# Two-layer gated network behind top-32 attention on one Trainium2 core: softmax weights turned by a transposing DMA, and five chunks instead of six

## The chip, the core and the metric

The program runs on one core of a Trainium2 chip. The metric is the device time of one execution in microseconds, the median of several runs. The engines are named as the profile has them: PE (TensorE, with PEld for its weight loads), DVE (VectorE), ACT (ScalarE), POOL (GpSimd) and SP (SyncE, which here issues every DMA).

## The reference

For 4 batches, 8 heads, 576 positions and a head width of 64, each row of scores keeps its 32 largest values and takes a softmax over them; the result is multiplied with v. The 2304 tokens of width 512 then go through two gated networks of inner width 1536, the first with silu, the second with a sigmoid as its gate.

```python
scores = scale * np.matmul(q, k.transpose(0, 1, 3, 2))
kth = np.partition(scores, -top_k, axis=-1)[..., -top_k:-top_k + 1]
scores = np.where(scores >= kth, scores, -1000000000.0)
attn = softmax(scores); x = np.matmul(attn, v)
g = x @ w_gate; x = (silu(g) * (x @ w_val)) @ w_out
x = (sigmoid(x @ w_gate2) * (x @ w_val2)) @ w_out2
```

## The kernel before, in words

The 36 units of 64 query positions (9 in each batch) are cut into chunks by `SIZES`, before `[4, 5, 6, 7, 7, 7]`; a chunk has an attention part (`attention`, `segment`) and a feed-forward part (`moe`). Heads go in four pairs. In `segment` two units of one batch make a *pair of row tiles*: two tiles of 128 rows by 576 scores, one for each head. A unit left over makes one tile (m = 1).

For each row tile `row_tile` finds the 32 largest values on DVE (`top_full`: four MAX8, three MATCH_REPLACE8), takes the exponent on ACT, and normalises on ACT or POOL. The weights `p` are then turned for the product with v: `turned` (L893) has PE transpose five 128-column blocks of a tile into PSUM (nine blocks for a pair), and ACT copies them into `pt` (L930). `pv` (L934) multiplies; PE's `ps_v` matmuls are the weighted sums. `pt` has one buffer (`PT = 1`).

Chunk 0 is in mode N: its feed-forward part multiplies in plain fp32, and its weights come from DRAM as 64-bit values, which `decode` (L513) turns to fp32 on ACT, POOL and DVE in four steps (L521 to L554). Every decoded piece is also stored to DRAM (`sw`, L557). All other chunks are in mode P: `slab` (L570) loads a decoded piece of weights again (`raw`), and `split_ops` (L497) splits it into a rounded high part (ACT or POOL) and a rest (POOL); activations are split likewise. Each product then takes three matmuls, high by high, high by rest and rest by high. A feed-forward part of a chunk in mode P is 864 matmuls over as many columns as the chunk has tokens, 64 for each unit. Its scores come from `stacked` and `stacked_scores` (L675), which stack high parts and rests, from pair of heads 1 of chunk 2 on; ahead of that, scores are plain fp32 (`score_ops`, L692).

The order on each engine is fixed in advance: `Plan` (L135) holds every operation with its estimated duration and a priority from the tables at the head of the file, places them one after another, and the program is then emitted in that order. So each engine, and SP's DMA queue, works strictly in order. Buffers are rings (`Ring`), and an operation that takes a buffer waits until its last user is done.

Of the kernel before, what the change touches and what calls it, by code (L numbers as in the profile page):

```python
# [9 lines left out]
F32 = mybir.dt.float32  # L10
# [42 lines left out]
DL = 6
NA = [0, 2, 3.5, 3.5, 4.0, 3.5]
NP = [1, 1, 1, 0, 2, 0]
P_XC = [0, 1, 0.5, 1, 0, 1]
P_EV = [0.5, 2, 1, 1, 1, 1]
D_WR = 10.5
D_ST = 5.5
D_RAW = [6, 4, 2.5, 0, 0, 0]  # L60
D_K = [0, 1, 1, 2, 0, 1]
D_V = [3.5, 1, 5.5, 3.5, 1, 3.5]
P_ROUND = [4, 4, 6, 4, 4, 4]
P_MASK = [0, 2, 0, 1, 1, 1]
P_DEC = 1.0
# [5 lines left out]
P_EX = [3.5, 3.5, 1.5, 2.5, 0, 0]
P_S = [0, 0, 0.5, 0.5, 1.5, 1.5]
P_X = [2, 2.5, 0.5, 1.5, 3.0, 1.5]
P_HH = [0, 0, 2.5, 0, 1.0, 2.0]
P_HL = [3, 1.5, 0, 0, 2, 1]
# [264 lines left out]
def attn_moe_kernel(ctx: ExitStack, tc, qT, kT, qD, kD, vL, wall, outT):  # L340
# [52 lines left out]
    def home(nm, dtype=F32):  # L393
# [5 lines left out]
        "x32": ring("x32", [P, NPAIR, S], F32, 1),  # L399
# [7 lines left out]
        "pt": ring("pt", [P, 9, 64 * GMAX], F32, PT),  # L407
        "v": ring("v", [P, 10, D], F32, V_RING),
# [56 lines left out]
    R["se", 0] = slot("xs", [P, 2, 2, 288], F32, 2)  # L465
    last = PHASE[-1]
    R["w", last] = Ring(lambda nm: [home(f"w_{4 * int(nm.split('_')[1]) + i}", F32R) for i in range(4)], WF // 4)
    R["w", last].before = lambda i: [g for k in range(4) for g in R["wf", 0].last(4 * i + k)]
    R["raw", last] = slot(lambda i: f"wr{i}" if i < WR else f"wu{i - WR}", [P, 512], F32, WR + WU)
    R["raw", last].before = lambda i: R["wr", 0].last(i) if i < WR else R["wu", 0].last(i - WR)  # L470
# [99 lines left out]
    def slab(c, i):  # L570

        mode, ph = MODES[c], PHASE[c]
        mode = {"a": "PS", "b": "SR"}.get(mode, mode * 2)[i % 2]
# [10 lines left out]
        w = new(("w", ph))  # L584

        def part(a, x):
            return w[2 * a + x][:].rearrange("p (a b) -> p a b", b=P)

        def block(x):
            return lambda a, d: part(a, x)[:, d]  # L590
        out = []
        for x in range(2):
            if mode == "R":
                ops = []
                for a in range(2):
                    def fn(a=a, x=x):
                        take(w)
                        nc.sync.dma_start(f32(part(a, x)), parts[i][a, x].rearrange("p (a b) -> p a b", b=P))
                    ops.append(op("dma", dma(128 * 2048), fn, deps=[kept[i][a, x]], allocs=[w], prio=4, lat=DMA_LAT))
                out.append((block(x), w, ops))  # L600
                continue
            r = new(("raw", ph))
            ld = load(r, scr32[i][:, x], n_bytes=128 * 2048, prio=D_RAW[now[0]], deps=stored[i])
            ops = split_ops(lambda x=x: part(0, x), lambda x=x: part(1, x),
                            lambda r=r: r[:].rearrange("p (a b) -> p a b", b=P), 512, [r], [ld], 2, 2, allocs=[w])
            for a in range(2 * (mode == "S")):
                def fn(a=a, x=x):
                    nc.sync.dma_start(parts[i][a, x].rearrange("p (a b) -> p a b", b=P), f32(part(a, x)))
                kept[i][a, x] = op("dma", dma(128 * 2048), fn, deps=[ops[a]], uses=[w], prio=6, lat=DMA_LAT)
            out.append((block(x), w, list(ops)))  # L610
# [23 lines left out]
    def stacked(bp, q0, n):  # L634
# [20 lines left out]
        lds.append(op("dma", dma(P * n * 256), fn, deps=lds, uses=[qr], prio=1, lat=DMA_LAT))  # L655
# [113 lines left out]
    def segment(c, p, b, q0, n_s, x32g, col, held=None):  # L769
# [123 lines left out]
    def turned(pg, norms, ptg, c0, k3, m):  # L893
# [39 lines left out]

    def pv(ptg, pt_ops, vg, v_ld, n, p, x32g, col):  # L934
# [232 lines left out]
```

## Time and profile before

| | |
|---|---|
| median of 3 runs | 1261.97 us (1261.35 to 1262.12) |
| the profiled execution | 1261.78 us, of which 1260.0 us are the span |
| PE, PEld busy | 1212.7 us (96%), 1060.8 us (84%) |
| DVE, ACT, POOL busy | 855.5, 874.7, 1047.0 us (68%, 69%, 83%) |
| DMA | 200.37 MB, mean 159 GB/s |
| clock granted to TensorE | 0.995 of full |

Times are counted from the start of the span. A busy time is the union of an engine's instructions, so neighbours that overlap count once. In a timeline row the start is measured, while ends of matmuls are modelled: the price of a matmul in a row of others is read from start to start. Register, semaphore and DMA-issuing instructions are not counted as busy.

### The profile page before, as it was taken

How to read it: one execution, taken by the hardware profiler on the slowest of the kernel's cores; microseconds unless marked ns; L12 is line 12 of the kernel's file. 1: busy time of each engine (PE TensorE's matmuls, PEld its weight loads, DVE VectorE, ACT ScalarE, POOL GpSimd, SP SyncE). 2: the span in 40 equal slices, each digit the busy share in tenths (PEclk: the TensorE clock that was granted, in tenths of full speed). 3: DMA queues.
4: the chain of work that ended last, by engine and by line, in shares of the span. 5: the costliest groups of instructions: out<-in, count | busy, mean ns of one | idle time of the engine just before them, and what ended most of it. 6: DMA issues, size and time to landing. Idle time of an engine off the chain costs nothing. (4 is left out here: it accounts for less than half of the span.)

```text
span 1260.0 us, 21906 instructions
## 1 busy us (share of the span) xinstructions
PE 1212.7 (96%) x7288; PEld 1060.8 (84%) x7288; DVE 855.5 (68%) x1872; ACT 874.7 (69%) x1886; POOL 1047.0 (83%) x1134
## 2 busy tenths in 40 slices
PE   4798999999999999999999999999999999999998
PEld 1376767879989899999998889999888899999998
DVE  6999999946999989999877999801968010121110
ACT  5998999967998999889888875434787433232331
POOL 5777989989999999979898887897887589787883
PEclk9899999999999999999999999999999999999999
DMA  7877788886444463544454464234232234333231
GB/s 262 261 265 255 256 279 273 265 261 192 139 150 142 135 209 114 163 132 142 129 169 139 142 220 152 98 121 131 78 105 68 84 105 137 112 112 117 100 106 41
DMA packets 100913, 200.37 MB, mean 159 GB/s; under 512 B 12480, under 2 KB 22848, under 8 KB 100800
## 3 DMA queue, kind: packets, MB, share of 16 engines
q1 hardware_dynamic: 100800, 198.98, 49.6%
q8 instruction: 57, 0.93, 0.3%
q14 instruction: 56, 0.46, 0.1%
HBM read 171.21 MB, written 27.72 MB: 158 GB/s over the span
## 5 line engine op out<-in xcount | busy, mean ns | idle before, releaser
L506 POOL TENSOR_TENSOR w<-raw,w 128x512 fp32r<-128x512 f32 x360 | 462.0, 1294 | 18.0 <-ACT w L501 5.6
L984 PE MATMUL ps_m<-xh,w 128*128 128x448 f32 (+2 forms) x1920 | 402.4, 351 | 1.5 <-DVE sil L955 1.4
L984 PEld LDWEIGHTS ps_m<-xh,w 128*128 128x128 f32 x1920 | 336.4, 188 | 21.2 <-issue 2.5
L882 DVE MAX8 st<-wk 128x8 f32<-128x576 f32 x432 | 313.2, 748 | 0.9
L984 PE MATMUL ps_m<-xl,w 128*128 128x448 f32 (+2 forms) x960 | 216.8, 347 | 0.0
L884 DVE MATCH_REPLACE8 wk<-st,wk 128x576 f32<-128x576 f32 x288 | 213.1, 742 | 0.0
L984 PE MATMUL ps_m<-hh,w 128*128 128x448 f32 (+2 forms) x960 | 199.2, 349 | 0.0
L984 PEld LDWEIGHTS ps_m<-xl,w 128*128 128x128 f32 x960 | 172.2, 187 | 8.7
L984 PEld LDWEIGHTS ps_m<-hh,w 128*128 128x128 f32 x960 | 168.8, 188 | 7.8 <-issue 0.4
L501 ACT ACTIVATE w<-raw 128x512 fp32r<-128x512 f32 x247 | 150.7, 625 | 20.2 <-PE ps_m L984 8.2
L506 POOL TENSOR_TENSOR hl<-h,hh 128x448 fp32r<-128x448 f32 (+2 forms) x120 | 128.8, 1074 | 5.6 <-ACT hh L501 5.0
L501 ACT ACTIVATE hh<-h 128x448 fp32r<-128x448 f32 (+2 forms) x116 | 62.9, 542 | 101.0 <-DVE h L955 67.8
L503 POOL TENSOR_SCALAR w<-raw 128x512 fp32r<-128x512 f32 x113 | 69.9, 619 | 67.1 <-PE ps_m L984 66.5
L842 ACT ACTIVATE e<-s,st 128x576 f32<-128x576 f32 x144 | 110.0, 771 | 19.8 <-DVE st L882 19.4
L955 DVE SCALAR_TENSOR_TENSOR h<-sil,ps_m 128x448 f32<-128x448 f32 (+2 forms) x60 | 34.5, 575 | 130.9 <-PE ps_m L984 126.6
L955 DVE SCALAR_TENSOR_TENSOR sil<-sil,ps_m 128x448 f32<-128x448 f32 (+4 forms) x83 | 40.6, 490 | 120.7 <-ACT sil L1019 120.7
L882 DVE MAX8 st<-s 128x8 f32<-128x576 f32 x144 | 106.0, 747 | 20.9 <-ACT s L702 20.8
L924 PE MATMUL ps_t<-ident,p 128*128 128x128 f32 x656 | 103.1, 284 | 16.9 <-POOL p L864 9.4
L930 ACT ACTIVATE pt<-ps_t 128x512 f32<-128x512 f32 (+4 forms) x288 | 112.2, 419 | 9.4 <-PE ps_t L924 7.8
L924 PEld LDWEIGHTS ps_t<-ident,p 128*128 128x128 f32 x656 | 76.8, 143 | 43.8 <-POOL p L864 19.8
L846 ACT ACTIVATE p<-e,st 128x576 f32<-128x576 f32 x144 | 110.8, 771 | 1.4 <-POOL st L837 0.6
L1019 ACT ACTIVATE sil<-ps_m 128x448 f32<-128x448 f32 (+4 forms) x155 | 71.6, 462 | 54.0 <-PE ps_m L984 53.5
(67 smaller groups left out, 1870.9 us busy)
## 6 DMA issues: line engine op xcount, KB each, us to landing
raw<-sw SPq DMA_DIRECT2D x360, 256.0 KB, 2.9
wr<-in_wall_dram SPq DMA_DIRECT2D x72, 512.0 KB, 4.8
sw<-wf SPq DMA_DIRECT2D x72, 256.0 KB, 3.2
kr<-in_kD_dram SPq DMA_DIRECT2D x42, 288.0 KB, 2.9
v<-in_vL_dram SPq DMA_DIRECT2D x34, 320.0 KB, 3.9
ss<-se SPq DMA_DIRECT2D x6, 576.0 KB, 3.6
s<-ss SPq DMA_DIRECT2D x6, 576.0 KB, 4.5
k<-in_kT_dram SPq DMA_DIRECT2D x11, 288.0 KB, 3.7
```

The costliest lines, as they stand in the source:

```text
L501: nc.scalar.activation(out=hi(), in_=raw(), func=AF.Copy)
L503: nc.gpsimd.tensor_scalar(hi(), raw(), 1.0, 1.0, op0=ALU.mult, op1=ALU.mult)
L506: (nc.gpsimd if eng == "pool" else nc.vector).tensor_sub(lo(), (lo_raw or raw)(), lo_hi() if lo_hi else f32(hi()))
L842: nc.scalar.activation(out=eg[:], in_=src(), func=AF.Prelu, bias=stg[:, 31:32], scale=-1.0, alpha=1.0 / STEEP)
L846: nc.scalar.activation(out=pg[:, e * S:(e + 1) * S], in_=eg[:], func=AF.Exp, bias=stg[:, 32:33], scale=-STEEP, accum_out=stg[:, 33:34])
L882: nc.vector.max(out=stg[:, 4 * k:4 * k + 8], in_=src() if k == 0 else fresh[:])
L884: nc.vector.match_replace(out=fresh[:], in_to_replace=stg[:, 4 * k - 4:4 * k + 4], in_values=src() if k == 1 else fresh[:], imm_value=NEG)
L924: nc.tensor.transpose(tg[:width, i], pg[:, a:a + width], ident)
L930: nc.scalar.activation(out=dst(), in_=src(), func=AF.Copy)
L955: nc.vector.scalar_tensor_tensor(out=out, in0=t, scalar=1.0, in1=x, op0=ALU.add, op1=ALU.mult)
L984: nc.tensor.matmul(pg[:, :n], blk(a, d), src(x, d), start=first and i == 0, stop=last and i == 4 * len(terms) - 1)
L1019: nc.scalar.activation(out=sg[:, :n], in_=pg[:, :n], func=AF.Tanh, scale=0.5)
```

## The change

Three things change together, and the tables of priorities with them.

**Chunks.** `SIZES` becomes `[4, 8, 8, 8, 8]`. Chunk 0 stays; then come four chunks of 512 tokens instead of five of 320, 384 and three times 448. A feed-forward part in mode P is run four times instead of five.

**Weights' buffers.** `raw` is loaded once for both halves of a slab (512 KB, ring of 3), and the split weights lie in a ring of `WH = 7` halves, each half a buffer of its own. The rings `sil`, `h32` and `wk` have one buffer fewer each.

**Turning.** From the third chunk on (`XT = "00111"`) a pair of row tiles is not turned on PE. `crossed` copies its fp32 weights on DVE, ACT or POOL into two planes of 16-bit halves, stores these to DRAM, and loads them back into `pt` by a DMA with `transpose=True`, which puts the two halves of each value next to each other again. A row tile left alone (m = 1) is turned as before. The blocks of `pt` are renumbered (0 to 3, 5 to 8, the shared one 4). 44 pairs are crossed: 16, 12 and 16 in chunks 2, 3 and 4.

```diff
-SIZES = [4, 5, 6, 7, 7, 7]
+SIZES = [4, 8, 8, 8, 8]
-MODES = "NPPPPP"
+MODES = "NPPPP"
-EARLY = '000002'
+EARLY = '00001'
-P_PT = [0.5, 3.5, 2.5, 2.5, 2.5, 5.5]
-P_PV = [1.5, 1, 0, 2, 0, 0]
+P_PT = [2.5, 3.5, 1.5, 1.5, 1.5, 4.5]
+P_PV = [1, 0, 0, 2, 0, 0]
...
-SIL = 4
-H32 = 3
-WK = 3
+WH = 7
+SIL = 3
+H32 = 2
+WK = 2
...
+XT = "00111"
+XT_NS = 4000.0
+PL = {'dve': (1270, 5), 'act': (1365, 6), 'pool': (1230, 4)}
+PL_DMA = 3.5
+PL_RING = 1
...
+        "pl": ring("pl", [P, 2 * S], F32, PL_RING, dt=I16),
...
-        w = new(("w", ph))
+        r = new(("raw", ph))
+        ld = load(r, scr32[i], n_bytes=128 * 4096, prio=D_RAW[now[0]], deps=stored[i])
         for x in range(2):
-            r = new(("raw", ph))
-            ld = load(r, scr32[i][:, x], n_bytes=128 * 2048, prio=D_RAW[now[0]], deps=stored[i])
+            w = new(("w", ph))
...
+                if XT[c] == "1" and m == 2:
+                    pt_ops.append(crossed(pg, norms, ptg, 2 * jp * 64))
+                    continue
                 for k3 in range(m + 1):
                     pt_ops += turned(pg, norms, ptg, 2 * jp * 64, k3, m)
...
+    def crossed(pg, norms, ptg, c0):
+        plg = new("pl")
+        scr = drp.tile([P, 2, 2 * S], I16, tag=plg.name, name=f"sp_{plg.name}")
+        ops = []
+        for e, d in enumerate(norms):
+            def plane(eng, e=e):
+                take(plg)
+                o = plg[:][:, :, e * S:(e + 1) * S]
+                i = pg[:, e * S:(e + 1) * S].bitcast(I16).rearrange("p (k t) -> p t k", t=2)
+                if eng == "act":
+                    nc.scalar.activation(out=o, in_=i, func=AF.Copy)
+                elif eng == "dve":
+                    nc.vector.tensor_copy(o, i)
+                else:
+                    nc.gpsimd.tensor_copy(o, i)
+            ops.append(op(PL, 0, plane, deps=[d], uses=[pg], allocs=[plg]))
+        def st():
+            nc.sync.dma_start(scr, plg[:])
+        a = op("dma", dma(P * 2 * S * 4), st, deps=ops, uses=[plg], prio=PL_DMA, lat=DMA_LAT)
+        def tr():
+            take(ptg)
+            nc.sync.dma_start(ptg[:, :, c0:c0 + P].bitcast(I16), scr.rearrange("q t k -> (q t) k"), transpose=True)
+        return op("dma", XT_NS, tr, deps=[a], allocs=[ptg], prio=PL_DMA, lat=DMA_LAT)
```

**The order on three engines.** In the rows below a name's number is that of its buffer's use, `x4` the number of like instructions in a row.

PE in the middle of chunk 1's second network, beside which the attention of chunk 2 runs (`ps_t` a transpose, `ps_m` a feed-forward product, `ps_v` a weighted sum). Before:

```order
490 L924 MATMUL ps_t_4897<-ident,p_4803 128x128 x4
491 L984 MATMUL ps_m_4906<-xh_4039,w_4643 128x320 x4
492 L984 MATMUL ps_m_4906<-xh_4039,w_4645 128x320 x4
493 L984 MATMUL ps_m_4906<-xl_4040,w_4643 128x320 x4
494 L924 MATMUL ps_t_4933<-ident,p_4803 128x128 x4
495 L984 MATMUL ps_m_4942<-xh_4039,w_4644 128x320 x4
496 L984 MATMUL ps_m_4942<-xh_4039,w_4646 128x320 x4
497 L984 MATMUL ps_m_4942<-xl_4040,w_4644 128x320 x4
498 L924 MATMUL ps_t_4963<-ident,p_4803 128x128
499 L984 MATMUL ps_m_4965<-xh_4039,w_4747 128x320 x4
```

and in the changed program:

```order
491 L1018 MATMUL ps_m_5260<-xh_4611,w_w_5013 128x512 x4
492 L1018 MATMUL ps_m_5260<-xh_4611,w_w_5014 128x512 x4
493 L1018 MATMUL ps_m_5260<-xl_4612,w_w_5013 128x512 x4
494 L1018 MATMUL ps_m_5291<-xh_4611,w_w_5070 128x512 x4
495 L1018 MATMUL ps_m_5291<-xh_4611,w_w_5071 128x512 x4
496 L1018 MATMUL ps_m_5291<-xl_4612,w_w_5070 128x512 x4
497 L977 MATMUL ps_v_5322<-pt_5244,v_4950 64x128 x10
498 L1018 MATMUL ps_m_5345<-xh_4611,w_w_5102 128x512 x4
499 L1018 MATMUL ps_m_5345<-xh_4611,w_w_5103 128x512 x4
500 L1018 MATMUL ps_m_5345<-xl_4612,w_w_5102 128x512 x4
```

The transposes between the products are gone, the products are 512 columns wide, and the weighted sum reads a `pt` that no PE instruction has prepared.

DVE at the place where chunk 1's feed-forward part starts. Before, its last native row tiles end, three decode steps follow, and then come the gates of chunk 1:

```order
419 L882 MAX st_2959<-wk_2985 128x8
420 L857 RECIPROCAL st_2902<-st_2902 128x1
421 L857 RECIPROCAL st_2959<-st_2959 128x1
422 L551 SCALAR_TENSOR_TENSOR wf_3065<-wf_3065,wu_305 128x512
423 L551 SCALAR_TENSOR_TENSOR wf_3080<-wf_3080,wu_328 128x512
424 L551 SCALAR_TENSOR_TENSOR wf_3103<-wf_3103,wu_366 128x512
425 L955 SCALAR_TENSOR_TENSOR sil_3215<-sil_3215,ps_m_3174 128x320
426 L959 TENSOR_TENSOR h_4_3239<-sil_3215,ps_m_3200 128x320
```

In the changed program `RECIPROCAL st_3331` closes the last row tile of chunk 1, and tiles of chunk 2 go on around it:

```order
475 L888 MAX st_3369<-wk_3385 128x8
476 L888 MAX st_3436<-s_3280 128x8
477 L890 MATCH_REPLACE wk_3385<-st_3369,wk_3385 128x576
478 L890 MATCH_REPLACE wk_3450<-st_3436,s_3280 128x576
479 L863 RECIPROCAL st_3331<-st_3331 128x1
480 L888 MAX st_3369<-wk_3385 128x8
481 L888 MAX st_3436<-wk_3450 128x8
482 L888 MAX st_3480<-s_3377 128x8
483 L890 MATCH_REPLACE wk_3450<-st_3436,wk_3450 128x576
484 L890 MATCH_REPLACE wk_3493<-st_3480,s_3377 128x576
```

Ahead of this place DVE has 48 row tiles of chunks 0 and 1 instead of 36, and 27 decode steps instead of 30.

SP's queue just behind the start of chunk 1's feed-forward part, with the semaphores that each issue waits for (`sp` the planes in DRAM, `kr` and `qr` keys and queries, `sw` the decoded weights in DRAM). Before:

```order
200 L494 DMA raw_3155<-sw_64 128x512 [waits DMAHW7_49,DVE_49]
201 L494 DMA raw_3163<-sw_65 128x512 [waits DMAHW0_49,Pool_49]
202 L494 DMA raw_3166<-sw_65 128x512 [waits DMAHW1_49,Pool_49]
203 L494 DMA raw_3187<-sw_66 128x512 [waits DMAHW4_49,DMAHW2_49,Pool_49]
204 L494 DMA raw_3193<-sw_66 128x512 [waits DMAHW5_49,DMAHW3_49,Pool_49]
205 L557 DMA sw_97<-wf_3103 128x512
206 L494 DMA raw_3219<-sw_67 128x512 [waits DMAHW6_49,Pool_49]
```

and in the changed program:

```order
215 L960 DMA sp_pl_174<-pl_3543 128x2304 [waits DMAHW6_49,Pool_49]
216 L652 DMA qr_3642<-in_qD_dram 128x128 [waits DMAHW4_49,DMAHW7_49,DMAHW2_49,Pool_49]
217 L513 DMA raw_3665<-sw_68 128x1024 [waits DMAHW0_49,Pool_49]
218 L513 DMA kr_3676<-in_kD_dram 128x576 [waits DMAHW5_49,Pool_49]
219 L656 DMA qr_3642<-in_qD_dram 128x128
220 L965 DMA_TRANSPOSE pt_3707<-sp_pl_174 128x9x256 [waits DMAHW6_49,DMAHW3_49]
221 L513 DMA raw_3752<-sw_69 128x1024 [waits Pool_49]
222 L960 DMA sp_pl_175<-pl_3669 128x2304 [waits Pool_49]
223 L513 DMA raw_3797<-sw_70 128x1024 [waits Pool_49]
224 L965 DMA_TRANSPOSE pt_3707<-sp_pl_175 128x9x256 [waits DMAHW7_49,DMAHW5_49]
225 L513 DMA raw_3865<-sw_71 128x1024 [waits DMAHW0_49,Activation_49,Pool_49]
226 L960 DMA sp_pl_176<-pl_3822 128x2304 [waits DMAHW1_49,DVE_49,Activation_49]
```

Between the loads now stand a store for each crossed pair, which waits for the engines that wrote the planes, and its transposing load, which waits for that store to land; weight loads (`raw`) stand behind both.

## Rows read from the trace of the kernel before

**Rows 1.** Timeline of PE, 255 to 275 us: start us, us, engine, line, operation.
```profile
273.08 1.44 PE L984 MATMUL ps_m<-xh,w 128*128 128x320 f32 x8
```

**Rows 2.** Busy time by stretch: PE, PEld, DVE, ACT, POOL, granted clock, DMA share, GB/s.
```profile
0.00:50.00 50.00, 25.63 (x197) 10.36 (x198) 39.91 (x87) 35.59 (x69) 29.54 (x45) 0.99 0.80 268
50.00:240.00 190.00, 180.19 (x1280) 131.40 (x1278) 180.87 (x419) 176.33 (x388) 158.93 (x194) 0.97 0.81 264
240.00:273.10 33.10, 31.79 (x171) 24.97 (x169) 23.45 (x46) 27.51 (x61) 26.18 (x32) 1.00 0.85 267
273.10:1256.00 982.90, 975.04 (x5647) 894.03 (x5645) 611.24 (x1322) 634.67 (x1370) 832.33 (x865) 1.00 0.42 130
1256.00:1260.00 4.00, 0.02 (x1) 0.00 (x0) 0.00 (x0) 0.54 (x1) 0.00 (x0) 1.00 0.15 57
```

**Rows 3.** Line L984 alone, 1000 to 1100 us: PE, PEld, clock, DMA.
```profile
1000.00:1100.00 100.00, 100.00 (x498) 93.01 (x497) 1.00 0.35 115
```

**Rows 4.** Timeline of PE, 400 to 440 us.
```profile
405.55 0.29 PE L675 MATMUL ps_s<-kh,qs 128*128 128x288 f32 x1
...
406.08 1.34 PE L984 MATMUL ps_m<-xh,w 128*128 128x320 f32 x8
...
414.93 0.71 PE L924 MATMUL ps_t<-ident,p 128*128 128x128 f32 x5
415.39 1.42 PE L984 MATMUL ps_m<-xh,w 128*128 128x320 f32 x8
416.65 0.75 PE L984 MATMUL ps_m<-xl,w 128*128 128x320 f32 x4
...
422.96 1.33 PE L984 MATMUL ps_m<-hh,w 128*128 128x320 f32 x8
424.14 0.75 PE L984 MATMUL ps_m<-hl,w 128*128 128x320 f32 x4
```

**Rows 5.** PE's groups, 273.1 to 1256 us: busy us, mean ns | idle before, releasers.
```profile
L924 PE MATMUL ps_t<-ident,p 128*128 128x128 f32 (+1 forms) x465 | 69.5, 276 | 4.7 <-POOL p L864 2.2 <-ACT pt L930 1.3 <-ACT p L862 0.6
L943 PE MATMUL ps_v<-pt,v 128*64 128x192 f32 (+5 forms) x462 | 60.6, 408 | 0.0
...
L984 PE MATMUL ps_m<-hn,wf 128*128 128x256 f32 x8 | 1.9, 379 | 0.0
```

**Rows 6.** Timeline of DVE, 235 to 290 us.
```profile
236.49 0.41 DVE L955 SCALAR_TENSOR_TENSOR hn<-sil,ps_m 128x256 f32<-128x256 f32 x1
236.81 0.09 DVE L884 MATCH_VALUE_LOAD wk<-st,s 128x8 f32 x1
...
237.54 0.76 DVE L882 MAX8 st<-s 128x8 f32<-128x576 f32 x1
238.21 0.75 DVE L882 MAX8 st<-wk 128x8 f32<-128x576 f32 x1
```

**Rows 7.** DVE's groups by shape, the whole span.
```profile
L551 DVE SCALAR_TENSOR_TENSOR wf<-wf,wu 128x512 int32<-128x512 int32 x30 | 25.4, 847 | 7.1 <-POOL wu L546 4.4 <-DMA raw<-sw 2.3 <-ACT wu L544 0.2
```

**Rows 8.** ACT's groups by shape, the whole span.
```profile
L842 ACT ACTIVATE e<-s,st 128x576 f32<-128x576 f32 x144 | 110.0, 771 | 19.8 <-DVE st L882 19.4
L702 ACT ACTIVATE s<-ps_s 128x576 f32<-128x576 f32 x116 | 74.6, 643 | 13.6 <-PE ps_s L692 8.4 <-PE ps_s L675 4.2
...
L535 ACT ACTIVATE wu<-wr 128x512 f16<-128x512 int16 x72 | 56.5, 785 | 2.2 <-POOL wu L460 1.5 <-DMA wr<-in_wall_dram 0.6
...
L709 ACT ACTIVATE s<-ps_s 64x288 f32<-64x288 f32 x56 | 22.4, 401 | 0.7 <-PE ps_s L675 0.2
```

**Rows 9.** DMA issues: count, KB each, median us from issue to landing.
```profile
ss<-se SPq DMA_DIRECT2D x6, 576.0 KB, 3.6
s<-ss SPq DMA_DIRECT2D x6, 576.0 KB, 4.5
...
qr<-in_qD_dram SPq DMA_DIRECT2D x10, 32.0 KB, 2.8
```

**Rows 10.** SP's waits: us in total, times, longest us.
```profile
SPq L494 <- POOL w L506: 522.8, 243, 9.8
```

More of the change, by code (lines that the diff above doesn't have):

```diff
@@ L40 @@
 PRE_PRIO = 3
-EARLY = '000002'
-E_FIRST = 0
-E_STEP = 0
-E_SKIP = 2
+EARLY = '00001'
+E_FIRST = 2
+E_STEP = 1
+E_SKIP = 3
 E_LAST = 1
-E_IN = [1, 2, 0, 0, 0, 0]
+E_IN = [0, 0, 2, 0, 0, 0]
 WR = 3
 E_PRIO = 0
-E_DMA = 5.5
+E_DMA = 4.0
 WU = 3
 KE = 2
-HP = 10
+HP = 1
 DL = 6
[L54 to L65, printed above, removed]
-P_MM = [5, 4.5, 7, 5.5, 6, 6]
-P_QK = [0, 1, 1.0, 1, 1, 1.5]
-P_K = [2, 1, 1.5, 1.5, 0, 5]
-P_PT = [0.5, 3.5, 2.5, 2.5, 2.5, 5.5]
-P_PV = [1.5, 1, 0, 2, 0, 0]
[L71 to L75, printed above, removed]
+NA = [0, 2, 2, 2, 2.5, 3]
+NP = [0, 0, 0, 0, 0, 0]
+P_XC = [0, 3, 0.5, 1, 1, 1]
+P_EV = [1, 1, 1, 1, 1, 1]
+D_WR = 11
+D_ST = 2.5
+D_RAW = [6, 6, 2.0, 2.5, 2.0, 2.5]
+D_K = [0, 1, 0, 1, 2, 0]
+D_V = [5.5, 1.5, 6.0, 3.5, 2.5, 3.5]
+P_ROUND = [4, 4, 6, 4, 4, 2]
+P_MASK = [3, 2, 2, 2, 1, 1]
+P_DEC = 1.5
+P_MM = [5, 4.5, 7, 5.5, 6, 6]
+P_QK = [0, 1, 3.5, 1.5, 1.0, 3.5]
+P_K = [1, 1, 0, 2.5, 1, 5]
+P_PT = [2.5, 3.5, 1.5, 1.5, 1.5, 4.5]
+P_PV = [1, 0, 0, 2, 0, 0]
+P_EX = [1.5, 3.5, 1.5, 1.5, 0, 0]
+P_S = [0.5, 0, 2, 0, 3, 1]
+P_X = [1, 0.5, 1, 0, 1.5, 0]
+P_HH = [0.5, 1, 0, 0, 0, 0]
+P_HL = [3, 0, 0, 2, 4, 2]
 PT = 1
-WF = 16
-XF = 8
+WF = 12
+XF = 12
+WH = 7
 W = 4
-SIL = 4
-H32 = 3
-WK = 3
+SIL = 3
+H32 = 2
+WK = 2
 E_RING = 2
@@ L360, in ring @@
             pl = pool(name, bufs, space)
+            if dt is not None:
+                return Ring(lambda nm: pl.tile([P, 2, shape[1]], dt, tag=name, name=nm), bufs)
             return Ring(lambda nm: pl.tile(shape, dtype, tag=name, name=nm), bufs)
@@ L464, in attn_moe_kernel, with w_tiles @@
     R["wu", 0] = Ring(still_tile, WU)
-    R["se", 0] = slot("xs", [P, 2, 2, 288], F32, 2)
+    R["se", 0] = slot("xs", [P, 2, 2, 288], F32, 2, xs_pool)
     last = PHASE[-1]
[L467 to L470, printed above, removed]
+    w_home = [("wf", i) for i in range(WF)] + [("wu", i) for i in range(WU)]
+    def w_tiles(nm):
+        out = []
+        for k in range(2):
+            kind, i = w_home[2 * (int(nm.split("_")[1]) % WH) + k]
+            out.append(home(f"w_{i}_{nm}", F32R) if kind == "wf" else
+                       arena.tile([P, 512], F32R, tag=f"wu{i}", name=f"w_{i}_{nm}", bufs=1))
+        return out
+    R["w", last] = Ring(w_tiles, WH)
+    R["w", last].before = lambda i: [g for k in range(2) for g in R[w_home[2 * i + k][0], 0].last(w_home[2 * i + k][1])]
+    R["raw", last] = slot("wr", [P, 2, 512], F32, WR)
+    R["raw", last].before = lambda i: R["wr", 0].last(i)
     for i, nm in enumerate(("xh", "xl")):
-        R[nm, last] = slot(lambda _, i=i: f"xs{i}", [P, ND, TP], F32R, 1)
+        R[nm, last] = slot(lambda _, i=i: f"xs{i}", [P, ND, TP], F32R, 1, xs_pool)
         R[nm, last].before = lambda _, i=i: R["se", 0].last(i)
@@ L583, in slab, with part @@
             return out
-        w = new(("w", ph))
[L586 to L590, printed above, removed]
         out = []
+        r = new(("raw", ph))
+        ld = load(r, scr32[i], n_bytes=128 * 4096, prio=D_RAW[now[0]], deps=stored[i])
         for x in range(2):
[L593 to L601, printed above, removed]
-            r = new(("raw", ph))
-            ld = load(r, scr32[i][:, x], n_bytes=128 * 2048, prio=D_RAW[now[0]], deps=stored[i])
[L604 to L610, printed above, removed]
+            w = new(("w", ph))
+            def part(a, w=w):
+                return w[a][:].rearrange("p (a b) -> p a b", b=P)
+            ops = split_ops(lambda part=part: part(0), lambda part=part: part(1),
+                            lambda x=x: r[:][:, x].rearrange("p (a b) -> p a b", b=P), 512, [r], [ld], 2, 2, allocs=[w])
+            out.append((lambda a, d, part=part: part(a)[:, d], w, list(ops)))
         return out
@@ L943, in go @@
                     nc.tensor.matmul(og[64 * h:64 * h + 64, :W], vg[:, 8 + h if i == 4 else 4 * h + i],
-                                     ptg[:, 8 if i == 4 else 4 * h + i, :W], start=(i == 0), stop=(i == 4))
+                                     ptg[:, 4 if i == 4 else 5 * h + i, :W], start=(i == 0), stop=(i == 4))
         a = op("pe", 200 + 10 * max(W / 1.2 + 3, 130), go, deps=pt_ops + [v_ld], uses=[ptg, vg], allocs=[og], prio=P_PV[now[0]])
```

41 lines of the change are left out of this document (21 added, 20 removed).

## Prediction

> **What bounds the kernel now.** I read the stretches of the span first. From 273.1 us, when the first matmul of chunk 1's feed-forward part starts [rows 1], until 1256 us TensorE is busy 975.0 of 982.9 us at full clock [rows 2]: there it is the bound, and only work taken off it, or run faster on it, counts. Ahead of that no engine is full. In 50 to 240 us PE is busy 180.2 of 190, VectorE 180.9 (0.952), ScalarE 176.3 (0.928), and the DMA engines have a share of 0.81 [rows 2]; 72 weight pieces are decoded there, and the attention of chunks 0 and 1 is worked off. So the time is three terms: the moment **T1** at which chunk 1's feed-forward part starts (273.1), what PE has to do behind it (982.9), and a tail of 4.0 us with PE idle [rows 2]; 1.8 us lie outside the span. The sum is made against the profiled execution's 1261.78 us; the median of the three runs, 1261.97, is 0.2 us above it.
>
> **The term behind T1: PE's work.** (a) The four split chunks have 3456 matmuls of 512 columns where 2592 of 448, 864 of 384 and 864 of 320 stood: the same columns, 864 matmuls fewer. The 448 form takes 100/498 = 0.2008 us [rows 3]; eight of 320 take 424.14 - 422.96 = 1.18, so 0.1475 each [rows 4]. That is 0.0267 for 64 columns, so 384 takes 0.1741 and 512 takes 0.2275, an extrapolation. Before: 520.5 + 150.4 + 127.4 = 798.3; after: 786.2. **-12.1.**
> (b) PE transposes. Behind T1 stand 465 [rows 5]; in the changed order 40, because 44 pairs of row tiles with nine each go to the DMA queue, and some single tiles move. Five of them start at 414.93, the eight matmuls behind start at 415.39 and take 1.26 instead of 1.18 [rows 4]: 0.54 for five, 0.108 each, from start to start. Ends: 0.092 without the slower matmul, and 69.5/465 = 0.149 of busy time [rows 5]. I take 0.108, the price of the place: 425 x 0.108. **-45.9** (-39 to -63). The 4.7 us of idle ahead of them [rows 5] go with them: **-4.3.**
> (c) 352 score matmuls instead of 392; four take 406.08 - 405.55 = 0.53 [rows 4]: **-5.3.** Eight matmuls of chunk 0 that ran behind T1 are due before it: **-1.9** [rows 5].
> (d) The weighted sums (PV, 60.6 us for 462 [rows 5]) become 480 of fewer columns: I take nothing, with 2.4 either way. What is late next is not PE's.
> Sum: 982.9 - 69.5 = 913.4.
>
> **The term T1 gets worse.** Chunk 1 now has eight units instead of five, and all its attention runs beside the decoding. VectorE, up to the last reciprocal of chunk 1 in the changed order: 196 MAX8 by 0.67 (238.21 - 237.54), 148 MATCH_REPLACE8 with their loads by 0.73 (237.54 - 236.81) [rows 6], 27 decode steps by 0.80, between their mean of 0.847 [rows 7] and the 0.07 that neighbours overlap, 12 gate steps of 256 columns by 0.32 [rows 6] 48 of half that width by 0.2, and 3 for the reciprocals: 277 us. It had done 39.9 at 50 us [rows 2]; the rest at 0.952 gives 299. Behind the last reciprocal come normalisation, five turns and their copies, the weighted sum and the split: 9 us. T1 = 308. ScalarE, counted apart: 239 us up to T1 before [rows 2], plus 8 row tiles by 2 x 0.771 = 12, evictions of scores 10 x 0.64 + 16 x 0.40 - 4 x 0.64 = 10 [rows 8], and some 50 small operations, an estimate of 13: 275; the rest beyond 35.6 at 0.928 gives 308. I take **308.5**, 35.4 later. Ends: VectorE never idle, 296; both engines at 0.88, 322. In return VectorE has row tiles of chunk 2 to work on at T1, where its queue had run dry before.
>
> **Costs taken at nothing, and their cover.** The crossing of one pair: 88 plane copies of 1152 elements, on three engines. No row shows one; the ScalarE row with 16-bit input takes 0.785 for 512 [rows 8], so 1.8 us, or 1.5 by twice a 576-wide pass. ScalarE gets 44, VectorE 21, GpSimd 23, and loses with them its copies from PSUM, GpSimd 72 weight splits. VectorE, the fullest, has after T1 some 95 row tiles by 4.96 (4 x 0.67 + 3 x 0.73 and a reciprocal) = 471, 120 gate steps at the pace of a 576-wide pass, 0.67, and 21 planes by 1.5: 583 us of the 717 until the last feed-forward part starts. If that cover fails, each plane costs 1.8 once. Then a store and a transposing load of 576 KB each. A plain store of that size lands in 3.6 us, a plain load in 4.5 [rows 9]; call the transposing load **X**. Lower end 4.5; upper end 18 squares of 32 KB one after another at the 2.8 us of a 32 KB load [rows 9], 50 us. I take 4.5 to 6: it moves the same bytes on the same queue.
> The Trainium skill ("Advanced Engine Details and Errata", X-Bar Transpose (TRN2)) says that such transfers go about as fast as plain ones; by that the sum stands. It says the opposite in "VectorE: DVE Perf Modes", The three transpose paths: 1309 ns for a 128x128 square. As an estimate that is 23.6 us for 18, and 1613 us in all by the rival's formula below. No run here shows either.
> SP's queue holds each transposing load behind a wait for its store, and weight loads behind that. SP's waits for freed weight buffers, 522.8 us in all, cost nothing today [rows 10]; three slabs of raw and three and a half of split weights lie ahead, each good for 24 x 0.2275 = 5.5 us of PE. If that cover were gone, 44 x 3.6 = 158 us would show.
>
> **Sum:** 308.5 + 913.4 + 4.0 = 1225.9, and 1.8 outside: **1227.7 us**, 34 less. Own range 1206 to 1246, by T1 (-13, +13) and the transposes (-17, +7).
>
> **Rivals.** (1) *Slower: the crossing sets the pace.* One buffer holds the turned weights, so a chunk needs 16 X + 8 x 2.6 (a weighted sum: 60.6 us over 23 of them). PE's own stretch for a chunk is 197 + 21 + 21 = 239. From X = 13.6 PE waits for the attention; each further microsecond costs 32 in chunks 2 and 4 together, and from X = 14.7 the gain is gone. At X = 20: 1228 + 205 + 22 (chunk 3, 12 crossings) = 1455. For it: nothing in the trace crosses, and 50 us lies far beyond. Against: 576 KB land in 4.5, and the DMA share behind T1 is 0.42 [rows 2], room for 52 MB more. Chance 0.17, SP's blocked weight loads included. (2) *The weighted sums wait at the head of PE's queue.* Planes, store and load take some 12 us where three turns and copies took 3; PE runs in order, so a late one stops the matmuls behind it. At 1 us for each of 24: 1252. Against: VectorE runs ahead of PE, and a wait once taken moves PE back for all later ones. Chance 0.13, for 1246 to 1259. (3) *The start eats the gain:* decoding and attention disturb each other, the two engines fall to 0.82, and T1 is 342: about 1262. Against: 0.93 and 0.95 today. Chance 0.05. (4) The transfer could run as a plain strided copy, so that the crossbar does nothing; that is rival 1 at its far end.
>
> **How the numbers follow.** The forecast has 0.62, a time under 1206 (T1 at 296 with the dear transposes gives 1198) 0.03, rival 2 0.13: faster by over 0.2% (2.5 us, about what a measurement of this kernel can tell from no change) has their sum, 0.78. Same 0.05, slower 0.17. The range goes from 1198 to 1268, where the nearest part of rival 1 ends.
>
> **What would show it.** Right: the first 512-column matmul at 300 to 320 us, eight of them in 1.82 us, PE above 98% busy from there, some 40 transposes behind it, transposing loads landing within 8 us. Wrong: PE idle ahead of weighted sums with a DMA as releaser (rival 2, or 1 if over 10 us each), idle ahead of weight matmuls with the raw loads late, or T1 beyond 330.

## The result, and the profile after

The changed kernel takes 1221.99 us (median of 4 runs, 1221.71 to 1222.36), the kernel before 1261.66 beside it (4 runs, 1257.38 to 1262.12). The ratio is 0.9695, 95% interval 0.968 to 0.9711: faster by 3%. The prediction was 1227.7, range 1198 to 1268. The profiled execution took 1221.71 us, 1219.9 of them in the span.

The stretches of the span, cut as in [rows 2] (PE, PEld, DVE, ACT, POOL, granted clock, DMA share, GB/s):

```profile
0.00:50.00 50.00, 28.03 (x185) 12.48 (x186) 41.99 (x91) 35.45 (x67) 31.43 (x47) 0.93 0.81 265
50.00:240.00 190.00, 176.77 (x1302) 131.48 (x1301) 185.29 (x426) 181.02 (x415) 157.14 (x179) 0.99 0.81 267
240.00:295.40 55.40, 49.90 (x336) 34.40 (x335) 55.40 (x126) 53.30 (x130) 42.19 (x52) 1.00 0.64 209
295.40:1215.80 920.40, 911.15 (x4329) 727.16 (x4328) 586.14 (x1212) 585.36 (x1145) 714.58 (x677) 1.00 0.58 166
1215.80:1219.90 4.10, 0.03 (x1) 0.00 (x0) 0.00 (x0) 0.60 (x1) 0.00 (x0) 1.00 0.18 66
```

Three terms again: T1 is 295.4 instead of 273.1, 22.3 later; the part behind it is 920.4 instead of 982.9, 62.5 less; the tail is 4.1. T1 is read in PE's timeline, as in [rows 1]:

```profile
295.44 0.96 PE L1018 MATMUL ps_m<-xh,w_w 128*128 128x512 f32 x3
297.51 1.43 PE L1018 MATMUL ps_m<-xh,w_w 128*128 128x512 f32 x5 [1.10 <-POOL xh L522]
```

PE's groups behind T1, which answer to [rows 5]. 465 transposes have become 40, and the weighted sums (L977) have no idle time ahead of them:

```profile
L977 PE MATMUL ps_v<-pt,v 128*64 128x256 f32 (+5 forms) x481 | 59.7, 394 | 0.0
L678 PE MATMUL ps_s<-kh,qs 128*128 128x288 f32 x176 | 51.7, 309 | 2.6 <-ACT s L705 2.5
...
L930 PE MATMUL ps_t<-ident,p 128*128 128x128 f32 (+1 forms) x40 | 6.4, 295 | 3.2 <-ACT p L868 3.1
```

All that PE waits for there (releaser, us in total, times, longest us), 9.0 us, and never for a DMA:

```profile
PE ps_t L930 <- ACT p L868: 3.1, 1, 3.1
PE ps_s L678 <- ACT s L705: 2.5, 6, 1.0
PE ps_s L678 <- POOL kl L525: 2.3, 4, 1.0
PE ps_m L1018 <- POOL xh L522: 1.1, 1, 1.1
```

The feed-forward matmuls alone, 1019 to 1215.8 us, as in [rows 3] (PE, PEld, clock, DMA): 196.80/859 = 0.2291 us for 512 columns.

```profile
1019.00:1215.80 196.80, 196.80 (x859) 160.87 (x857) 1.00 0.29 88
```

The crossing. First the instructions by tile (duration in ns, min/median/max; first and last start), then the issues with KB and us to landing, beside [rows 9]:

```profile
L960 SPq DMA_DIRECT2D sp_pl<-pl x44: 337/344/1499, 301.4 to 902.5; - x44
L965 SPq DMA_TRANSPOSE pt<-sp_pl x44: 2287/3120/4487, 307.4 to 905.9; - x44
L952 ACT ACTIVATE pl<-p x44: 1145/1152/1169, 305.8 to 897.9; 128x1152 int16<-128x1152 int16 x44
L956 POOL COPY pl<-p x23: 1141/1144/1160, 294.0 to 861.4; 128x1152 int16<-128x1152 int16 x23
L954 DVE COPY pl<-p x21: 736/1174/1976, 324.8 to 898.7; 128x1152 int16<-128x1152 int16 x21
```

```profile
sp_pl<-pl SPq DMA_DIRECT2D x44, 576.0 KB, 3.7
pt<-sp_pl SPq DMA_TRANSPOSE x44, 5.3
```

A plane takes 1.15 us (median), the store lands in 3.7, the transposing load in 5.3.

### The profile page after: what moved, and what is told of

Read it like the earlier page. It is cut to its first block, busy times and chain, and to the rows that moved or that the text cites. A ratio compares the mean times of both kernels' runs of the same rounds, so it can differ in the third digit from the quotient of the medians.

```text
span 1219.9 us, 18873 instructions
## 1 busy us (share of the span) xinstructions
PE 1165.9 (96%) x6148; PEld 905.5 (74%) x6148; DVE 868.8 (71%) x1852; ACT 855.7 (70%) x1756; POOL 945.3 (77%) x954
## 5 line engine op out<-in xcount | busy, mean ns | idle before, releaser
L525 POOL TENSOR_TENSOR w_w<-raw,w_w 128x512 fp32r<-128x512 f32 x288 | 374.7, 1307 | 116.6 <-ACT w_w L520 110.8
L1018 PE MATMUL ps_m<-xh,w_w 128*128 128x512 f32 x1536 | 385.0, 393 | 1.1 <-POOL xh L522 1.1
L1018 PEld LDWEIGHTS ps_m<-xh,w_w 128*128 128x128 f32 x1536 | 284.2, 188 | 61.3 <-POOL xh L522 1.5
L520 ACT ACTIVATE w_w<-raw 128x512 fp32r<-128x512 f32 x214 | 132.9, 624 | 124.1 <-PE ps_m L1018 71.0
L1018 PE MATMUL ps_m<-xl,w_w 128*128 128x512 f32 x768 | 207.3, 392 | 0.0
L1018 PE MATMUL ps_m<-hh,w_w 128*128 128x512 f32 x768 | 192.2, 392 | 0.0
L1018 PEld LDWEIGHTS ps_m<-xl,w_w 128*128 128x128 f32 x768 | 144.3, 188 | 31.7
L1018 PEld LDWEIGHTS ps_m<-hh,w_w 128*128 128x128 f32 x768 | 142.8, 188 | 30.8 <-issue 0.7
L525 POOL TENSOR_TENSOR hl<-h,hh 128x512 fp32r<-128x512 f32 x96 | 125.5, 1307 | 3.4 <-ACT hh L520 2.0
L848 ACT ACTIVATE e<-s,st 128x576 f32<-128x576 f32 x144 | 110.5, 769 | 15.9 <-DVE st L888 15.7
L890 DVE MATCH_REPLACE8 wk<-st,s 128x576 f32<-128x576 f32 x144 | 106.5, 740 | 0.0
L977 PE MATMUL ps_v<-pt,v 128*64 128x128 f32 (+6 forms) x800 | 92.7, 377 | 0.2 <-ACT pt L936 0.2
```

Source lines behind the costliest of these rows:

```text
L520: nc.scalar.activation(out=hi(), in_=raw(), func=AF.Copy)
L525: (nc.gpsimd if eng == "pool" else nc.vector).tensor_sub(lo(), (lo_raw or raw)(), lo_hi() if lo_hi else f32(hi()))
L848: nc.scalar.activation(out=eg[:], in_=src(), func=AF.Prelu, bias=stg[:, 31:32], scale=-1.0, alpha=1.0 / STEEP)
L890: nc.vector.match_replace(out=fresh[:], in_to_replace=stg[:, 4 * k - 4:4 * k + 4], in_values=src() if k == 1 else fresh[:], imm_value=NEG)
L1018: nc.tensor.matmul(pg[:, :n], blk(a, d), src(x, d), start=first and i == 0, stop=last and i == 4 * len(terms) - 1)
```

## The experiments

The runs were compared with the kernel before beside them (1259.5 to 1260.5 us). The theory to begin with was the prediction's: the chunks by themselves do little, and the crossing takes the transposes off PE at no cost, because one crossing has room until it takes 13.6 us. One thing holds for all runs but two: an edit that takes operations away, adds some, or changes a price, a rank or a ring makes the planner write a new order on every engine, so a few microseconds of a difference can be the order's. Only the runs with two and three loads under point 4 keep the change's order.

**1. The new chunks without the crossing.**

```diff
-XT = "00111"
+XT = "00000"
```

> The changed kernel with all softmax weights turned on PE again (new chunks, no crossing). Theory (the gain is PE work taken off, 396 transposes by 0.108 us and their waits, while the new chunks alone nearly cancel: start 22 us later, products and scores 12 us less, the rest small): 1222 + 47 = about 1269 us, so no faster than the kernel before. Rival (the larger chunks carry the gain and the crossing is only a convenience): under 1240 us.

Measured: 1268.55 us (5 runs), ratio 1.007 (1.0048 to 1.0091). The theory held. So the chunks, with their tables and buffers, lose 9 us without the crossing, and the crossing is worth 46.6. Its PE behind T1 (which is 297.2), the whole stretch and the transposes:

```profile
296.00:1262.00 966.00, 955.09 (x4733) 766.65 (x4730) 566.11 (x1191) 583.23 (x1216) 691.97 (x671) 1.00 0.33 104
```

```profile
L930 PE MATMUL ps_t<-ident,p 128*128 128x128 f32 (+1 forms) x432 | 63.8, 276 | 2.4 <-POOL p L870 1.2 <-ACT p L868 0.9
```

Against the change, PE is busy 955.09 - 911.15 = 43.9 us more, with 392 transposes more: about 0.112 us each, where the prediction took 0.108.

**2. A plain load in place of the transposing one, and no planes.** What is left out is the turning: the weights are stored as they are and loaded back unturned.

```diff
-            nc.sync.dma_start(scr, plg[:])
+            nc.sync.dma_start(scr, pg[:])
...
-            nc.sync.dma_start(ptg[:, :, c0:c0 + P].bitcast(I16), scr.rearrange("q t k -> (q t) k"), transpose=True)
+            nc.sync.dma_start(ptg[:, :, c0:c0 + P], scr.rearrange("q (a b) -> q a b", a=9))
```

> The changed kernel without plane copies and with a plain load in place of the transposing one: the normalised weights go to DRAM and back unturned, so the turning is left out and the weighted sums of chunks 2 to 4 multiply unturned weights. Theory (planes and the transposing load are hidden behind PE): 1222 within 4 us. Rival (PE's waits of some 9 us behind the start, and the 88 copies of 1.15 us, come from the crossing): 1212 us or less.

Measured: 1219.99 us (4 runs), ratio 0.9681 (0.9659 to 0.9704), 2 us below the change. So the 88 planes and the turning in the load have together no price beyond some 2 us. The way through DRAM stays in this run; that it costs PE nothing in the change is told by PE's waits above, none of which ends with a DMA. The plain load lands no sooner than the transposing one:

```profile
pt<-sp_p SPq DMA_DIRECT2D x44, 576.0 KB, 5.3
```

**3. The old chunks, with and without the crossing.** Both have the sizes and tables of before and the new weight buffers.

```diff
-SIZES = [4, 8, 8, 8, 8]
+SIZES = [4, 5, 6, 7, 7, 7]
...
-XT = "00111"
+XT = "000000"
```

> The partner of the run before: six chunks, old tables, new weight buffers, no crossing. Theory (the weight buffers cost or give nothing): 1262 within 5 us. Rival (raw loads of 512 KB and seven half buffers give part of the gain): under 1250 us.

Measured without the crossing: 1259.87 us (10 runs), ratio 1.0001 (0.9989 to 1.0013). The weight buffers cost and give nothing. Then with `XT = "001111"`:

> Six chunks and the priority tables of the kernel before, the new weight buffers, and crossing from the third chunk on (48 pairs; one buffer fewer of sil). Theory: 432 transposes by 0.108 and 4 us of waits leave PE, the start stays at 273 us: 1262 - 51 = about 1211 us, faster than the changed kernel. Rival (crossing needs the larger chunks, or the old tables place it badly, so that PE waits for weighted sums): 1235 us or more.

Measured: 1273.26 us, ratio 1.0105 (1.0079 to 1.0131). The theory fell by 62 us: 48 pairs are off PE, and the kernel is slower. Two causes offered themselves. In chunk 2 the first crossings stand at about 240 us, inside the decoding, and PE's share falls there (240 to 300 us, columns as above):

```profile
240.00:300.00 60.00, 46.31 (x234) 36.13 (x233) 25.39 (x50) 35.52 (x69) 33.67 (x36) 0.89 0.85 263
```

In the same stretch the run without the crossing has PE at 57.41 us, clock 1.00 and a DMA share of 0.75. The first product of chunk 1's feed-forward part (T1), which the theory left at 273, comes 12.8 us later with the crossing than without it, nearly the whole loss of 13.4. The two lines, with the crossing and without:

```profile
282.22 0.94 PE L1018 MATMUL ps_m<-xh,w_w 128*128 128x320 f32 x4
269.43 1.44 PE L1018 MATMUL ps_m<-xh,w_w 128*128 128x320 f32 x8
```

So the meeting with the decoding costs the start, and behind it the crossing gains nothing either. For that the other cause could be the tables or the sizes. So two more runs. In the first, `XT = "000111"`:

> The chunks and tables of before (sizes 4, 5, 6, 7, 7, 7), with the crossing only from the fourth chunk on, that is after the weights are decoded. Theory A (the crossing lost with the old chunks because its planes and transfers met the decoding, in a stretch in which VectorE, ScalarE and the DMA engines have nothing to spare): with the meeting gone the 42 crossing pairs are worth what they are in the change, 42 of 44 times 46.6 us, so 1260 less 40 to 45, between 1213 and 1225 us. Theory B (the old tables or the small chunks give the DMA round trip too little time wherever it stands): TensorE waits for crossings or for what they delay in the later chunks too, and the time stays above 1245 us.

Measured: 1250.78 us (4 runs), ratio 0.9929 (0.9909 to 0.9949). By the rule written down theory B holds, yet leaving chunk 2 to PE gave back 22.5 us, 11.7 of them at T1 (270.5), so the meeting with the decoding has its price too. Only 36 pairs cross here, not the 42 of the expectation: 324 transposes at 0.112 should give 36 us. The stretch with the crossings, of this run and then of the one without:

```profile
440.00:980.00 540.00, 517.32 (x2894) 466.38 (x2893) 452.15 (x961) 422.22 (x854) 483.91 (x515) 0.98 0.75 214
```

```profile
440.00:980.00 540.00, 533.01 (x3147) 486.66 (x3147) 429.43 (x937) 419.34 (x914) 454.00 (x487) 1.00 0.41 135
```

PE idles 22.7 us instead of 7.0, and the clock is 0.98 instead of 1.00, as an estimate some 10.8 us of 540. 36.3 - 15.7 - 10.8 leaves 9.8; the medians differ by 9.1. From 300 to 1000 us PE's idle time lies in pieces of up to 2.6 us ahead of scores, feed-forward products and transposes, and none of it ends with a crossing: 10.5 us end with POOL (6.6 for `kl`, 2.9 for `w_w`), 14.5 with ACT. POOL is busy 0.896 of this stretch, ACT 0.782; in the change's (440 to 920 us) it is 0.826 and 0.762. Which of these loads is the cause is not shown; no run moved such work away.

The second took the tables of the change with the old sizes:

> The sizes of before (4, 5, 6, 7, 7, 7) with the tables of the change and the crossing from the third chunk on. Theory A (the meeting with the decoding): the third chunk's first crossings still stand before the decoding's end, so the time stays above 1240 us. Theory B (the tables were the cause, the sizes do not matter): 1222 within 10 us. No number of rows says which tables suit these sizes, so a result between 1232 and 1240 tells nothing.

Measured: 1294.4 us, ratio 1.027 (1.0252 to 1.0288). This says little, since those tables were made for other chunks. How much of the loss is the sizes' and how much the tables' stays open.

**4. How much room a crossing has.** Each transposing load is issued twice, then three times.

```diff
-            nc.sync.dma_start(ptg[:, :, c0:c0 + P].bitcast(I16), scr.rearrange("q t k -> (q t) k"), transpose=True)
+            for _ in range(2):
+                nc.sync.dma_start(ptg[:, :, c0:c0 + P].bitcast(I16), scr.rearrange("q t k -> (q t) k"), transpose=True)
```

> The change with each transposing load issued twice into the same tile, the second behind the first's landing, so that the crossing's last link takes about 5.3 us more on SyncE's queue. Theory (the crossings of a row block have slack, and one costs nothing until it takes 13.6 us): now about 3.7 + 2 times 5.3, the queue's own share about 10.6 us, under 13.6: 1222 to 1230 us. Rival (the products PV wait at the head of TensorE's queue as soon as the crossing is late): 44 pairs at up to 5.3 us each, 100 to 230 us more.

> The change with each transposing load issued three times into the same tile, each behind the landing of the one before. Theory (capacity at 13.6 us a crossing, 32 us of time for each us beyond): the queue's share is about 15.9 us, so some 74 us more, about 1296 us (1270 to 1330). Rival (the slack of the queue is larger, or the rows decide where TensorE has other work): under 1240 us.

Measured: 1337.2 us, ratio 1.0609 (1.0578 to 1.064), and 1541.48 us, ratio 1.2243 (1.2213 to 1.2272). The theory fell twice, by over 100 and some 245 us. PE behind T1, with two loads and with three:

```profile
296.20:1327.00 1030.80, 943.21 (x4344) 744.82 (x4341) 591.06 (x1214) 587.95 (x1147) 714.60 (x678) 0.96 0.63 173
```

```profile
296.00:1541.00 1245.00, 991.22 (x4325) 774.01 (x4326) 590.41 (x1212) 589.02 (x1145) 711.43 (x677) 0.88 0.62 164
```

With two, the 110 us over the change are 78 more of idle time (87.6 against 9.2) and 32 more of busy time for the same work: a part of the matmuls ran at the lower of the two clocks (1.2 instead of 2.4 GHz), and the granted clock of the stretch is 0.96 instead of 1.00. From two to three, 204 us for 44 loads are 4.64 us each. A load's landing there is 4.6: by then every crossing seems to be on the path with its whole length, and the slower matmuls (48 us more of busy time) run in its shadow.

Two explanations. In the change's timeline the 20 products with v begin 0.6 to 6.0 us (median 3.2) behind the landing of their last crossing; with two loads, 19 of 20 begin 0.2 us or less behind it (starts and landings read from the traces). So the lead that PE's fixed order gives may be all the room there is. The next run keeps two loads and tells the planner:

```diff
-XT_NS = 4000.0
+XT_NS = 9300.0
```

> The run with every transposing load issued twice took 1337.2 us, against 1222 of the change. Here the same two loads, with the planner's cost of a crossing raised from 4.0 to 9.3 us, so that it writes TensorE's order with the products PV some 5 us later. In the change's trace 20 products PV begin 0.6 to 6.0 us (median 3.2) behind the landing of their last crossing: the lead the order gives. Theory C (the lateness costs because the order's lead is short, and a later place costs nothing, since SyncE's queue has time up to 13.6 us a crossing): most of the 115 us come back, 1222 to 1250 us, and no long waits of ps_v for DMA. Rival (the queue or the DMA engines have no time for a second load, wherever PV stands): above 1300 us.

Measured: 1345.79 us, ratio 1.0687 (1.0669 to 1.0706). The lead came back (18 of 20 products begin 1.5 us or more behind the landing), and not one microsecond of time. Theory C fell. PE waits for a crossing once now (18.1 us), and for the rest mostly for ACT and POOL; its granted clock is 0.94 behind T1. The other explanation was the one buffer of planes, for which the engines waited 9.0 us in the change. With two loads the view of the planes' tile has this as the idle time ahead of them (releaser, us, times):

```profile
  DMA sp_pl<-pl: 105.9, 34
```

The last run gave it a second buffer:

```diff
-SIL = 3
-H32 = 2
+SIL = 2
+H32 = 1
...
-PL_RING = 1
+PL_RING = 2
```

> Two loads per crossing as in the run of 1337.2 us, with two buffers for the planes instead of one (paid for by one buffer less for sil and for h). In that run's trace the planes waited 105.9 us, 34 times, for the store of the pair before to land, against 9.0 us, 8 times, in the change's own; that store stands in SyncE's queue behind the pair before's two loads. Theory D (the one buffer ties each crossing to the one before it: planes, store, loads, then the next planes): with two buffers the planes run ahead, the waits for sp_pl go under 30 us, and at least half of the 115 us come back: under 1285 us. Rival (SyncE's queue alone, which the two loads hold for some 7 to 10 us each time, whatever buffer is free): the waits of the planes fall but the time stays between 1310 and 1345 us.

Measured: 1331.25 us, ratio 1.058 (1.0547 to 1.0613). The planes' wait fell to 1.5 us, and 6 us came back. Theory D fell; the rival's numbers held. SyncE's queue in this run (start us, us; x2 is a crossing's two loads):

```profile
421.43 0.37 SPq L960 DMA_DIRECT2D sp_pl<-pl  x1
421.85 0.42 SPq L513 DMA_DIRECT2D raw<-sw  x1
422.33 1.28 SPq L513 DMA_DIRECT2D v<-in_vL_dram  x1
425.77 9.25 SPq L966 DMA_TRANSPOSE pt<-sp_pl  x2
435.12 0.53 SPq L513 DMA_DIRECT2D kr<-in_kD_dram  x1
...
436.22 0.38 SPq L960 DMA_DIRECT2D sp_pl<-pl  x1
436.65 0.43 SPq L656 DMA_DIRECT2D qr<-in_qD_dram  x1
437.17 0.94 SPq L513 DMA_DIRECT2D raw<-sw  x1
439.98 7.77 SPq L966 DMA_TRANSPOSE pt<-sp_pl  x2
```

Store, wait for its landing, two loads held 8 to 9 us, and only then the next pair's store: 14.2 us from crossing to crossing, planes ready or not. From the first store to the last it is 699 us here (304.2 to 1003.6) and 601 in the change (301.4 to 902.5): 98 of the 109 us lost. SP's own waits show the queue held (us in total, times, longest us), first in the change, then in the run of 1337.2 us with its two loads:

```profile
SPq L965 <- DMA sp_pl<-pl: 28.2, 19, 3.5
```

```profile
SPq L966 <- DMA sp_pl<-pl: 103.2, 33, 7.1
SPq L966 <- DMA pt<-sp_pl: 91.5, 44, 3.5
```

That the queue's order is the whole of it is what is left after the lead and the buffer, not shown by a run of its own. In the run with the raised price, as the trace's order of stores and loads has it, 12 of 43 stores stand ahead of the loads of the pair before, without a gain, but there every engine has another order too. A run with all stores ahead of the loads and nothing else moved, or with the crossing on another queue, was not made.

**5. What sets T1.**

```diff
+        T = 23 if now[0] < 2 else 31
...
-        for k in range(2 * (TOPK // 8) - 1):
+        for k in range(5 if now[0] < 2 else 7):
```

> The change with only the 24 largest found in each row of the first two chunks (the fourth round left out, so its threshold is the 24th and those rows' weights differ). VectorE loses some 48 rounds of 0.73 + 0.74 us, about 67 us, ahead of the first product of the wide layer. Theory (VectorE alone sets the 295.4 us to that product; it is never idle from 240 us on): the end falls until ScalarE or the decoding stops it, 10 to 20 us off, 1202 to 1212 us. Rival (ScalarE, 0.95 busy there, or the decoding, which stands level with it): 1219 to 1223 us.

Measured: 1225.93 us, ratio 0.9735 (0.9719 to 0.9752). The theory fell: T1 is 297.3, not earlier; the rival's range is missed by 3 us. VectorE has room now, ScalarE has little (50 to 240 us, then up to T1):

```profile
50.00:240.00 190.00, 174.15 (x1321) 128.14 (x1315) 158.31 (x362) 179.24 (x418) 154.91 (x185) 0.96 0.78 256
240.00:297.30 57.30, 54.37 (x330) 40.71 (x328) 47.09 (x106) 55.81 (x134) 48.30 (x56) 1.00 0.74 249
```

ScalarE is 0.943 busy, then 0.974. But the new order also moved the decoding: its last fp32 products (`hn` by `wf`, chunk 0's) end at 293.6 us, in the change at 279.4. In the change, then in this run:

```profile
277.52 1.89 PE L1018 MATMUL ps_m<-hn,wf 128*128 128x256 f32 x8
284.76 8.80 PE L1019 MATMUL ps_m<-hn,wf 128*128 128x256 f32 x40
```

So here the end of the decoding stands 4 us ahead of T1, where in the change VectorE's last reciprocal does (289.39, below). Whether ScalarE's load or the planner's order put the decoding later is not shown. The other way round, nine of VectorE's decode steps were given to GpSimd (the second number is a rank in the planner's choice, the lower first):

```diff
-F4 = {"dve": (632, 2), "pool": (2280, 4)}
+F4 = {"dve": (632, 4), "pool": (2280, 2)}
```

> The change with the planner's liking for GpSimd raised in the last step of the decoding, so that 18 of the 72 decoding products stand on VectorE instead of 27, and 54 on GpSimd instead of 45. VectorE loses 9 times 0.89 us, 8 us, ahead of the first product of the wide layer, and GpSimd takes 9 times 2.37 us, 21 us. Theory (VectorE alone sets that end): 4 to 8 us faster, 1214 to 1218 us. Rival (GpSimd becomes the limit of the decoding): 1224 to 1235 us.

Measured: 1247.53 us, ratio 0.9907 (0.9892 to 0.9922). T1 went to 322.1, which is the whole of the 25.5 us lost; both sides of the expectation missed it. The decoding itself is slower, chunk 0's last fp32 products end at 309.0 (50 to 240 us):

```profile
50.00:240.00 190.00, 168.14 (x1247) 122.41 (x1240) 185.85 (x432) 172.53 (x391) 136.57 (x165) 0.91 0.71 229
```

The DMA share is 0.71 instead of 0.81, PE is 8.6 us less busy at a granted clock of 0.91 instead of 0.99, and GpSimd, which took the steps, is less busy too (136.57 instead of 157.14), though VectorE is as busy as before. In both runs the decoding ends later than in the change, by 14 and 30 us, and T1 comes no earlier. What sets the decoding's pace stays open; a few steps moved, with the new order that came of it, cost more than their length. No run that computes everything was faster than the change.

## Why the prediction was right

**T1: 308.5 predicted, 295.4 measured.** The work was counted well: up to chunk 1's last reciprocal VectorE was busy 276.7 us, where 277 were counted, and ScalarE up to T1 269.8, where 275 were. The reciprocal, and the stretch up to it (columns as in [rows 2]):

```profile
289.39 0.15 DVE L863 RECIPROCAL st<-st 128x1 f32<-128x1 f32 x1
0.00:289.40 289.40, 250.07 (x1778) 175.75 (x1778) 276.69 (x627) 264.62 (x597) 227.63 (x272) 0.98 0.79 258
```

The pace was the miss. I let VectorE go on at 0.952 and ScalarE at 0.928; they ran at 0.975 and 0.953 in 50 to 240 us, at 1.00 and 0.962 behind it. So the reciprocal came at 289.4 instead of 299, and 6.0 us lie behind it instead of 9. The time came out at the lower end, "VectorE never idle, 296". But that VectorE alone holds T1 is not borne out: with 37 us of its busy time gone, T1 stayed, while the decoding ended 14 us later in that run's order. Of the signs named, this one missed: the first 512-column product was to come at 300 to 320 us.

**Behind T1: 913.4 predicted, 920.4 measured.** (a) The product price, an extrapolation to 0.2275, is 0.2291: 3456 times 0.0016 is 5.5 us too little. (b) The transposes cost 0.112 by experiment 1 instead of 0.108, 1.7 us more gained. The idle time left is 9.2 us; 7.9 [rows 2] less the 4.3 taken away would have been 3.6, so 5.7 more than planned. Some 2.5 us the other way are not assigned. (d) The weighted sums: 59.7 us against 60.6 [rows 5], nothing, as taken.

**Sum.** T1 13.1 too late, the rest 7.0 too short, the tail 0.1 short: 1221.7 for the profiled run. The two misses have opposite signs, so that the total is better than its parts is luck. How the own range of 1206 to 1246 was made from its two terms is not told: their ends added give 1198 to 1248.

**Costs taken at nothing.** They were nothing, or 2 us at most: experiment 2 for the planes and the turning, PE's waits for the way through DRAM. The planes are 1.15 us, not 1.5 to 1.8. The transposing load lands in 5.3 us, inside the 4.5 to 6, and 45 below the upper end. SP still waits for freed weight buffers, 376.2 us in 104 times against 522.8 in 243 [rows 10], and PE never for a weight load behind T1: the cover held. The Trainium skill ("Advanced Engine Details and Errata", X-Bar Transpose (TRN2)) has such transfers go about as fast as plain ones; the traces agree, 5.3 beside 5.3 for the plain load of experiment 2. The Trainium skill's 1309 ns for a 128x128 square ("VectorE: DVE Perf Modes", The three transpose paths) doesn't carry over: 5.3 us for 18 squares are 0.29 each.

**Rivals.** Rivals 2 and 3 did not come: no DMA releases PE behind T1, and T1 lies below the forecast, not at 342. Nor did rival 4: 5.3 us is no far end. Rival 1 did not come either, but my step for it was wrong, "16 X + 8 x 2.6 ... from X = 13.6 ... each further microsecond costs 32". I left out the store, which stands ahead of the load in the same queue, and so gave the two an overlap that the order of the queue does not have. Store and loads together take, by their medians, 3.7 + 5.3 = 9.0 us in the change, 5.4 + 2 x 4.6 = 14.6 with two loads, 5.6 + 3 x 4.6 = 19.4 with three. The runs with two and three loads lie on (1541.5 - 1337.2)/4.8 = 43 us for a microsecond, which is one for each of the 44 pairs, not 32; drawn back to no loss, if it runs straight so far, that line starts at 14.6 - 115.2/43 = 11.9 us. As an estimate, the change has 2.9 us of room in each crossing, where I thought I had 7.6. By that estimate a transposing load of over 8.2 us would have met rival 1.

## What to carry to other kernels

Here work taken off the bound engine was worth its start-to-start price (0.112 us a transpose, 44 us in all) only where the detour fitted into every queue that it passed: the same detour lost 13 us where it met the decoding, gave 9 with the smaller chunks and old tables, and 46.6 where there was room. In a queue that runs in order, count the whole chain of a step (store, landing, load) against the time between two such steps, not the one transfer against an average. And when an engine reads as never idle, take some of its work away before calling it the bound, and look at what else the edit moved: here the time stayed, but the decoding had moved too.

## What the runs showed of the hardware

The issue of a transposing load holds SyncE's queue for 3.12 us (median of 44), that of a plain load of the same bytes for 0.53 (experiment 2), of a plain store for 0.344. The transposing loads go in small packets, and the share of the DMA engines is higher for the same bytes. First the change, then the plain load:

```profile
DMA packets 175170, 228.22 MB, mean 187 GB/s; under 512 B 112352, under 2 KB 117728, under 8 KB 175072
...
q1 hardware_dynamic: 175072, 227.02, 62.6%
```

```profile
DMA packets 123777, 228.21 MB, mean 187 GB/s; under 512 B 10272, under 2 KB 66336, under 8 KB 123680
...
q1 hardware_dynamic: 123680, 227.02, 57.9%
```

102,080 more packets lie under 512 bytes; 44 times 576 KB in pieces of 256 bytes would be 101,376. And a copy that reads every second 16-bit value takes about the same on three engines, medians of 1.14 to 1.17 us for 1152 elements; on VectorE single ones took 0.74 to 1.98.
